# Packed loads of a, q, k on one queue, v narrowed on the chip, states in two operations: a gated-attention and MLP kernel on one core

## The chip, the cores and the metric

The kernel runs on one core of a Trainium2 chip. The metric is the device time of one execution in microseconds; a profiled execution gives in addition a trace and a span (first to last instruction). Engines are TensorE (PE), its weight load (PEld), VectorE (DVE), ScalarE (ACT), GpSimd (POOL) and SyncE (SP). The program fixes the order of each engine's instructions.

## The reference, cut to what matters

```python
# q, k, v, alpha: [4 batches, 8 heads, 768 tokens, 48] f32
for t in range(S):
    state = alpha[:, :, t, :, None] * state + einsum('bhd,bhe->bhde', k[:, :, t], v[:, :, t])
    y[:, :, t] = einsum('bhd,bhde->bhe', q[:, :, t], state)
x = y as [3072 tokens, 384]
h = x @ w_in                                   # 384 -> 2048
g = 0.5 * h * (1 + tanh(sqrt(2/pi) * (h + 0.044715 * h**3)))
return g @ w_out                               # 2048 -> 384
```

## The kernel before

The tokens are cut in six chunks of 128, the four batches in two pairs, which gives twelve "pairs" (0 to 11), in the order chunk by chunk. For each pair the kernel loads a (alpha), q, k and v. It takes ln of a, sums it along the tokens with a matmul (`cum`), forms `b = exp(cum)` and its inverse, scales q and k with them (`qp`, `kp`) and transposes both. Then come the attention inside the chunk (`at`, masked to `atm`), y (`yps`), k-times-v for the carried state (`kv`), and the two layers of the MLP (`hT`, then `acc`).

Python code at build time lists tasks with assumed durations in ns (the table `W`), simulates the engines, and emits the instructions in the resulting order. So a duration in `W` costs nothing on the chip, but it decides the order. Parts that the change touches:

```python
W = dict(..., st=1400, st0=700, ..., strip=2120, cast=1500, ...)
LOADS = ('gatea0', 'v0', 'gatek0', 'in 0', 'pk1', 'in 1', 'in 2', 'v1', ...)   # POOL's loads, in order
RINGS = (('a', 0, 0, 'SP'), ('a', 0, 2, 'ACT'), ..., ('q', 1, 3, 'SP'))        # 20 pieces, on SP and ACT
BUFS = dict(..., ot=6, bend=8, a=4, q=4, k=4, v=6)
...
def load(self, n, c, i, lo=0, hi=2):            # v: f32 in memory, bf16 on chip, so a casting DMA
    ...
    u[n] = self.tile(n, [C, 2, H, D], BF16 if n == "v" else F32)
    (nc.sync if e == "SP" else nc.gpsimd).dma_start(...)
...
def carry(self, u, i, c, b):                    # state = (kv + old) * b at the chunk's end
    for o in range(2):                          # the two diagonal blocks of a head pair, 64 lanes each
        ps, fs = slice(64 * o, 64 * o + 64), slice(D * o, D * o + D)
        acc = kv[ps, :, fs]
        if c > 0:
            s = ...
            nc.vector.tensor_tensor(s[ps], acc, old[ps, :, fs], op=ALU.add)
            acc = s[ps]
        nc.vector.tensor_tensor(new[ps, :, fs], acc, u["bend"][ps, i, :, None].to_broadcast(...), op=ALU.mult)
```

A buffer is reused in turn: with `a=4` the a of pair 4 can be issued only when pair 0 is done with its a. `gatea0` is a tiny POOL copy that waits until a of pair 0 has landed and so holds back the loads behind it.

## Time and profile before

| | before |
|---|---|
| time, median of 3 runs | 185.55 us (184.06 to 185.78) |
| span of the profiled run | 183.2 us |
| v, k of pair 1, loads of later pairs, weights | POOL, 0.6 to 1.3 us of issuing each |
| loads of pairs 0 and 1 (a, q; k of pair 0) | SP and ACT, in pieces |

```profile
33.10 2.76 PE L516 MATMUL acc<-w_out,gT 128*128 128x384 bf16 x16
...
54.55 0.34 PE L441 MATMUL kv<-v,kp 128*128 128x96 bf16 x4
```

Apart from 0.4 us for gT, PE's waits lie in the first 24 us. No wait for `v` appears in that view.

### The profile page before, as it was taken

To read this page: it belongs to the slowest core of one execution; us is meant where nothing else is said; L and a number is where in the kernel's file an instruction comes from. 1 tells how busy PE (TensorE), PEld (TensorE's weight loads), DVE (VectorE), ACT (ScalarE), POOL (GpSimd) and SP (SyncE) were. 2 spreads that over 40 slices of the span, in tenths; PEclk is the share of its full clock that TensorE was granted. 3 is DMA by queue.
4 is the path that set the end of the run, shared out by engine and by line. 5 is a ranking of instruction groups with operands and counts; after the bars stand their busy time and mean duration, and the time that the engine had idled before them with its cause. 6 is when DMAs were issued, how large, how long until landed. Compare 5 with 4: busy or idle time off the path is not lost.

```text
span 183.2 us, 4630 instructions
## 1 busy us (share of the span) xinstructions
PE 175.7 (96%) x1861; PEld 129.3 (71%) x1861; DVE 104.2 (57%) x232; ACT 135.6 (74%) x310; POOL 60.9 (33%) x68
## 2 busy tenths in 40 slices
PE   7887999999999999999999999999999999999993
PEld 2465869666686787687688769678677677686873
DVE  7775954065969896597499798298644715000000
ACT  3666969873888789859799768899789884491941
POOL 2595837975545755564750200000000000000000
PEclk9999999999999999999999999999999999999999
DMA  5999999999999999999999955753271290311102
GB/s 155 187 242 211 187 231 214 204 202 174 195 281 183 169 229 197 181 225 205 180 213 235 179 171 100 104 115 67 52 170 46 43 202 4 88 43 47 43 0 86
DMA packets 51206, 27.76 MB, mean 151 GB/s; under 512 B 38833, under 2 KB 48241, under 8 KB 51185
## 3 DMA queue, kind: packets, MB, share of 16 engines
q0 software_dynamic: 32096, 17.70, 69.0%
q1 hardware_dynamic: 18512, 9.38, 21.5%
q10 hardware_dynamic: 576, 0.39, 0.7%
q8 instruction: 14, 0.23, 0.6%
q14 instruction: 8, 0.06, 0.1%
HBM read 25.17 MB, written 4.72 MB: 163 GB/s over the span
## 4 chain that ended last, share of the span: by engine, by line
PE 85%; DMA 6%; ACT 3%; DVE 2%; SPq 1%; ACTq 1%; issue 0%
PE acc L516 34%; PE hT L497 31%; PE at L424 4%; PE qkT_ps L364 4%; PE yps L473 3%; DMA a<-in_alpha_dram 2%; PE yps L470 2%; DMA q<-in_q_dram 2%; PE cum L320 2%; PE kv L441 2%; DMA qkT<-kp 2%; PE xT_ps L487 1%; DVE atm L431 1%; ACT L503 1%; PE cum L322 1%; SPq L247 1%
## 5 line engine op out<-in xcount | busy, mean ns | idle before, releaser
L497 PE MATMUL hT<-xT,w_in 128*128 128x256 bf16 x576 | 70.1, 273 | 0.4 <-ACT gT L503 0.4
L503 ACT ACTIVATE gT<-hT 128x256 bf16<-128x256 f32 x192 | 63.4, 387 | 8.6 <-PE hT L497 8.3
L516 PE MATMUL acc<-w_out,gT 128*128 128x384 bf16 (+1 forms) x400 | 68.8, 319 | 0.0
L497 PEld LDWEIGHTS <-w_in 128*128 128x128 bf16 x576 | 54.0, 98 | 8.0 <-issue 0.6
L516 PEld LDWEIGHTS <-gT 128*128 128x128 bf16 x400 | 36.8, 98 | 19.6
L431 DVE TENSOR_TENSOR atm<-at,ut 128x512 bf16<-128x512 f32 x48 | 30.9, 685 | 15.0 <-PE at L424 14.5
L354 DVE TENSOR_TENSOR qp<-q,b 128x768 bf16<-128x768 f32 (+1 forms) x15 | 11.7, 794 | 18.7 <-ACT b L343 15.8
L528 ACT COPY ot<-acc 128x384 f32<-128x384 f32 (+1 forms) x18 | 8.3, 462 | 13.9 <-PE acc L516 12.6
L235 POOL DMA_DIRECT2D v<-in_v_dram x13 | 14.6, 1123 | 9.6 <-PE hT L497 2.9
L235 POOL DMA_DIRECT2D k<-in_k_dram x11 | 12.2, 1112 | 11.0 <-DVE kp L354 5.2
L343 ACT ACTIVATE b<-cum 128x768 bf16<-128x768 f32 (+1 forms) x15 | 10.2, 684 | 6.7 <-PE cum L322 3.1
L235 POOL DMA_DIRECT2D q<-in_q_dram x11 | 12.3, 1114 | 7.0 <-DMA k<-in_k_dram 1.8
L235 POOL DMA_DIRECT2D a<-in_alpha_dram x11 | 12.3, 1114 | 5.9 <-ACT gT L503 2.2
L213 ACT ACT_TABLE_LOAD x9 | 11.5, 1283 | 2.8 <-issue 2.6
L480 ACT CAST x<-yps 128x384 bf16<-128x384 f32 x16 | 7.7, 481 | 7.8 <-PE yps L473 7.6
L458 DVE TENSOR_TENSOR st<-stmp,bend 64x192 bf16<-64x192 f32 x32 | 11.3, 353 | 1.5
L354 DVE TENSOR_TENSOR kp<-k,binv 128x768 bf16<-128x768 f32 (+1 forms) x15 | 11.8, 792 | 0.2
L456 DVE TENSOR_TENSOR stmp<-kv,st 64x192 f32<-64x192 f32 x32 | 11.3, 352 | 1.0 <-PE kv L441 0.7
L503 ACT ACT_TABLE_LOAD x9 | 11.5, 1283 | 0.2
L222 PE MATMUL idle<-zero 128*128 128x512 bf16 x27 | 9.5, 462 | 1.2 <-DVE blk L778 1.2
L382 DVE COPY qkT<-qkT_ps 128x1024 bf16<-128x1024 bf16 (+1 forms) x13 | 8.7, 688 | 3.0 <-PE qkT_ps L364 2.9
L343 ACT ACTIVATE binv<-cum 128x768 bf16<-128x768 f32 (+1 forms) x15 | 10.1, 683 | 0.0
(62 smaller groups left out, 159.4 us busy)
## 6 DMA issues: line engine op xcount, KB each, us to landing
out_dram<-ot SPq DMA_DIRECT2D x23, 192.0 KB, 2.3
a<-in_alpha_dram POOLq DMA_DIRECT2D x9, 384.0 KB, 13.1
q<-in_q_dram POOLq DMA_DIRECT2D x9, 384.0 KB, 13.2
k<-in_k_dram POOLq DMA_DIRECT2D x9, 384.0 KB, 13.3
v<-in_v_dram POOLq DMA_DIRECT2D x11, 192.0 KB, 13.3
w_in<-in_moe_w_in_dram POOLq DMA_DIRECT2D x4, 384.0 KB, 7.7
w_out<-in_moe_w_out_dram POOLq DMA_DIRECT2D x4, 384.0 KB, 9.8
a<-in_alpha_dram SPq DMA_DIRECT2D x6, 96.0 KB, 3.4
```

The lines of the kernel that those rows point to most:

```text
L213: nc.scalar.add_instruction(mybir.InstLoadActFuncSet(name=nc.get_next_instruction_name(), act_func_set_id=i, engine=mybir.EngineType.Activ ...
L222: self.nc.tensor.matmul(ps, self.zero[:, 0:self.C], self.zero, start=True, stop=True)
L235: (nc.sync if e == "SP" else nc.gpsimd).dma_start(u[n][:, lo:hi].rearrange("t b h d -> t (b h) d"), src)
L343: self.nc.scalar.activation(u[n].rearrange("t i h d -> t i (h d)")[:, lo:hi], cum, AF.Exp, scale=1.0 if n == "b" else -1.0)
L354: self.nc.vector.tensor_tensor(out, rows, b, op=ALU.mult)
L382: self.copy(e)(t, ps)
L431: self.nc.vector.tensor_tensor(u["atm", i][:, o], u["at", i][o], self.ut[:, None, :].to_broadcast([self.C, self.H // 2, self.C]), op=ALU.mult)
L456: nc.vector.tensor_tensor(s[ps], acc, old[ps, :, fs], op=ALU.add)
L458: nc.vector.tensor_tensor(new[ps, :, fs], acc, u["bend"][ps, i, :, None].to_broadcast([64, H // 2, D]), op=ALU.mult)
L497: self.nc.tensor.matmul(h, self.w_in[:, j, nt * self.C:(nt + 1) * self.C], self.xT[c][:, j, lo:hi].rearrange("p g t -> p (g t)"), start=j ...
L503: return lambda e: self.nc.scalar.activation(self.gT[c % self.NG][:, nt, lo * self.C:hi * self.C], f.pop(("h", c, lo, nt)), AF.Gelu_apprx_ ...
L516: self.nc.tensor.matmul(f["acc", c, b][:, lo:hi], self.gT[c % self.NG][:, nt, b * self.C:(b + 1) * self.C], self.w_out[:, nt, lo:hi], star ...
```

## The change

The intent is a shorter head. Of the first two pairs, a, q and k come in one transfer each on SP's queue, four tokens a row, instead of pieces. A casting load has to leave from GpSimd (point 1 of the prediction's section on the Trainium skill), so v of pair 0, now on SP, comes as f32; v of pairs 0 to 3 is f32 and a copy on chip (`vb`) narrows it to bf16: for pairs 0 and 1 on DVE, for pairs 2 and 3 on POOL. The state takes two operations over all 128 lanes instead of four over 64; a small operation (`ends`) multiplies the decay with a mask of zeros and ones, so that the unwanted blocks vanish. The scheduler's durations are adapted (`st`, `strip`, `cast` and others).

```diff
-    ... st=1400, st0=700, ...      strip=2120, cast=1500, ...
+    ... st=1090, st0=545, end=110, ... strip=1850, cast=3000, ... ring=1150, vb2_pool=950, ...
-    LOADS = ('gatea0', 'v0', 'gatek0', 'in 0', 'pk1', 'in 1', 'in 2', 'v1', 'in 3', ...)
+    LOADS = ('gatev0', 'in 0', 'v1', 'in 1', 'in 2', 'in 3', 'out 0', '2a', 'out 1', '2b', ...)
-    RINGS = (('a', 0, 0, 'SP'), ('a', 0, 2, 'ACT'), ... 20 pieces)
+    RINGS = (('a', 0), ('q', 0), ('k', 0), ('a', 1), ('v', 0), ('q', 1), ('k', 1))
+    NARROW = (0, 1, 2, 3)
-    BUFS = dict(... ot=6, bend=8, a=4, q=4, k=4, v=6)
+    BUFS = dict(... ot=5, bend=3, ends=8, a=4, q=4, k=4, v=2, vb=6)
...
+    def narrow(self, u, lo, hi):
+            (self.nc.gpsimd.tensor_copy if e == "POOL" else self.nc.vector.tensor_copy)(u["vb"]..., u["v"]...)
...
-            for o in range(2):
-                ... add and multiply on 64 lanes
+                nc.vector.tensor_tensor(s, acc, old, op=ALU.add)
+            nc.vector.tensor_tensor(new..., acc..., ends, op=ALU.mult)
...
+                    narrow[lo:hi] = [s.add("vb", {"DVE": W[f"vb{n}"]} if early else {"POOL": W[f"vb{n}_pool"]},
+                                           P + 9 if early else -1, self.narrow(u, lo, hi), [loads["v", m, lo]])] * n
```

Also changed: the setup of the small masks takes three operations instead of a dozen, the memsets of the states fall away, and `cum` of pair 0 takes a buffer apart from pair 1's.

## The prediction

> **What bounds the kernel now.** The page comes first: PE (TensorE) is busy for 96% of the 183.2 us span. The busy time of each engine in stretches then splits PE's time; its columns are the stretch, its length, and busy us (instructions) of PE, weight load, DVE, ACT and POOL, then granted clock, DMA share and GB/s.
>
> ```profile
> PE 175.7 (96%) x1861; PEld 129.3 (71%) x1861; DVE 104.2 (57%) x232; ACT 135.6 (74%) x310; POOL 60.9 (33%) x68
> ```
>
> ```profile
> 0.00:17.20 17.20, 13.47 (x128) 7.66 (x129) 11.96 (x50) 9.07 (x23) 9.94 (x21) 1.00 1.04 199
> 17.20:28.70 11.50, 11.24 (x142) 8.83 (x139) 8.10 (x18) 9.25 (x24) 7.59 (x10) 1.00 1.46 205
> 28.70:175.00 146.30, 145.76 (x1550) 108.78 (x1549) 84.17 (x165) 115.64 (x261) 43.39 (x39) 1.00 0.91 148
> ```
>
> The same view for the fill matmuls (tile "idle") gives 7.96, 1.19 and 0.38 us. So real PE work is 5.5 of the first 17.2 us, 10.05 of the next 11.5, and nearly all of the 146 us after. An improvement can come only from the first 28.7 us. A loss can come from anything that makes PE, which runs its instructions in order, wait later.
>
> The chain that ended last, in order of time, says what the head waits for (start, us, what):
>
> ```profile
> 1.68 3.91 DMA q<-in_q_dram
> 5.60 0.31 SPq L247
> ...
> 6.94 4.41 DMA a<-in_alpha_dram
> 11.45 0.53 ACT la L301
> ...
> 15.38 1.02 DVE qp L354 x2
> 16.41 0.28 DVE xT L491
> ```
>
> The SP queue issues a of pair 1 only when q of pair 0 has landed; a of pair 1 arrives at 11.35. The program order agrees: from the ninth hardware transfer on, each waits for the eighth before it. By issue plus time to landing, the last piece of q of pair 1 comes at 15.2. DVE is in order, so its scaling at 15.38 holds the two xT copies behind it, and layer 1 begins at 17.21.
>
> The POOL queue decides my number. Its timeline from 38 us (start, us, instruction, idle before):
>
> ```profile
> 40.52 1.16 POOL L235 DMA_DIRECT2D v<-in_v_dram  x1 [1.19 <-issue]
> 42.55 1.15 POOL L235 DMA_DIRECT2D a<-in_alpha_dram  x1 [0.87 <-issue]
> 44.71 1.15 POOL L235 DMA_DIRECT2D q<-in_q_dram  x1 [1.00 <-DVE atm L431]
> 46.13 1.15 POOL L235 DMA_DIRECT2D k<-in_k_dram  x1 [0.28 <-issue]
> 48.26 1.15 POOL L235 DMA_DIRECT2D v<-in_v_dram  x1 [0.98 <-issue]
> ...
> 61.66 1.15 POOL L235 DMA_DIRECT2D a<-in_alpha_dram  x1 [1.02 <-DMA k<-in_k_dram]
> 63.15 1.15 POOL L235 DMA_DIRECT2D v<-in_v_dram  x1 [0.34 <-PE acc L516]
> ```
>
> POOL issues one strip per 2.1 us, not per 1.15 us. Landings (issue plus time to landing of each single transfer) are: a of pair 3 40.2, q 42.2, k 44.4, v 45.8, then a of pair 4 48.0, up to v of pair 5 at 62.9. Each issue above follows by 0.3 us the landing of the transfer seven places before it: v of pair 4 at 40.52 after 40.2, a of pair 5 at 42.55 after 42.2, v of pair 8 at 63.15 after 62.9. POOL is held at the pace of the data. Today this is free, since only loads for later pairs stand in that queue.
>
> **What the Trainium skill says.** (1) "DMA: Bandwidth & Descriptors", section SWDGE vs HWDGE vs iDMA: a transfer that casts must be issued from GpSimd. The trace agrees, with every v on POOL at 192 KB against 384 KB of the others; so v on SP must stay f32, hence the copies. (2) "VectorE: DVE Perf Modes", section The TRN2 errata: an f32 tensor_tensor of N elements a lane takes (N+151)/0.96 ns. That is 357 for 192 and 557 for 384; the trace has 353 (st, 64x192) and 552 (kp, 128x384). (3) "GPSIMD Engine Reference", section 3.1: 1.8 cycles an element at 1.2 GHz as a best loop. I take from it an estimate of 0.58 us for a copy of 128x384 and 1.15 for 128x768; no such copy is in this trace. (4) "TensorE: Matmul & The Clock Gate", Part 1: after an idle window of about 3.4 us PE runs at half clock for about as long. The first nine fills agree (4.02 us, 0.45 each, against 0.22 modelled later); no later stall here is long enough to show it again.
>
> **The change part by part.**
>
> *Head.* Eight a/q pieces, four k and eight more of pair 1 on SP, ACT and POOL become seven transfers on SP with no slot wait (seven are under eight). Issues took 0.31 to 0.46 us, so all are out by about 3.9 us. The stretch from 2 to 3 us moved 284 GB/s, so 393 KB take 1.4 us: a of pair 0 at about 3.9, q 5.3, k 6.6, a of pair 1 8.0. For v, with 192-byte rows, I take 2.0 us (about 200 GB/s, the rate of such rows on POOL): 10.1. Then q at 11.5 and k at 12.9. q thus comes 3.7 us earlier than now. But DVE takes in v of pair 0 (two copies, 0.6) ahead of four masks (0.65 each, until about 13.6), then qp, xT, two kp, xT (0.55+0.35+1.05+0.35): layer 1 starts near 16.0, 1.1 us earlier.
>
> *States.* 72 operations of 0.353 us (25.4) become 36 of 0.557 plus ten ends of about 0.11 (21.2): 4.2 us off DVE, which is 57% busy and does not bound. PE idles only 0.54 us between 28.7 and 175 us, so this is worth at most a few tenths.
>
> *Narrowing.* For pairs 0 and 1 it is on DVE, 4 x 0.3. For pairs 2 and 3 the scheduler gave it to POOL, and the built program shows where:
>
> ```
> POOL: a3 q3 k3 v3 a4 q4 [narrow 2, first half] k4 v4 a5 q5 k5 [narrow 2, second half]
>       v5 a6 q6 k6 v6 v7 a7 v8 [narrow 3] ...
> PE:   y of pair 2, both halves, and kv of pair 3 wait for POOL
> ```
>
> Digits are pairs. The copy for pair 3 stands behind 19 loads, which POOL issues at the pace of landings. When does it run?
>
> - The first weight transfer is gated on v of pair 0 (10.1), so issued at 10.3 against 8.19 now, but with less beside it: landing about 15.0 (now 15.5). From there one queue. Landings now give 1.9 us a weight part, and 3.3 and 3.5 us for the two halves of pair 2; v in f32 adds 0.5 to each. Up to a of pair 3: seven weight parts 13.2, v of pair 1 1.9, pair 2 7.8, a of pair 3 2.1, or 25.0, so 40.0 (now 40.2).
> - v of pair 3 as f32 costs 0.6 more than as bf16. From a of pair 3 to v of pair 5 it was 22.7, so 23.3 now: 63.3. v of pair 8 is issued 0.3 later, and 1.15 + 1.15 us on the copy is done: **65.9**.
> - PE reaches kv of pair 3 at 54.55 now. In the new order six layer-1 matmuls (0.66 us) move behind it, and the head gives 1.1: 52.8 without stalls.
> - The second half of pair 2 waits as well: its copy stands behind k of pair 5, issued when v of pair 3 landed (46.2+0.3+1.15, plus the copy, 48.3). y needs it at 45.69 now, 44.6 then: 3.7 us of stall, so kv of pair 3 is reached at 56.5 and waits 9.4 more.
>
> The end moves by 65.95 - 54.55 + 0.66 = 12.1 us, since PE has no slack afterwards to win it back. A stall of 9 us ought to cost about 1.5 us of half clock besides. The gains at the head vanish: kv of pair 3 is tied to POOL, not to PE.
>
> **Rivals.** *A: the intended gain.* If the POOL copies come in time, only the head counts: -1.1 us, about 184.4. For it: the scheduler placed the copies so that they are in time by its own costs. Against it: those costs let POOL issue every 1.1 us, while the trace shows 2.1. *B: a milder POOL stall.* If transfers run faster with all hardware loads gone early (say 1.85 instead of 2.06 us a strip), the copy is done near 63 and the end moves by about 9 us. The strips after 38 us already run without competing loads, which speaks against much of this. *C: v of pair 0 late on the hardware queue.* It holds DVE and the gate of all weights; a microsecond late there delays layer 1 and, through the weights, the whole POOL queue by as much. That adds to my case. *D: DVE blocked by v of pair 1* (a copy waiting until about 17 us): at most 1 us, swallowed by the later wait.
>
> **How the numbers follow.** The span becomes 183.2 + 12.1 + 1.5 = 196.8; the timed median stands 2.35 above the span now, giving 199. I lean a little towards B and say 197.5. The low end, 190, is strips of 1.6 us from 39 us on (copy done at 59.8, end 5.9 later), no clock loss, and a time only 0.9 above the span, as in the fastest run; the high end, 203, is C on top. Rival A keeps 9 in 100, split between a small and a large gain.
>
> **What would show it.** Right: two POOL copies late, the one of 128x768 near 65 us; PE waiting on POOL for some 4 us before y of pair 2 (about 44 to 48) and 9 us before kv of pair 3 (about 57 to 66); a lower PE clock just after; a of pair 1 landed by about 8, layer 1 started near 16; state operations near 0.55 us. Wrong: that copy done before 55 us, no PE wait on POOL, and PE idle after 28 us still around half a microsecond; or strips landing clearly faster than one per 2 us.

## More of the kernel before

The prediction shows the busy line, three stretches, the chain of waits and POOL's timeline. What is to be added here is the view of waits for PE alone (engine, tile, source line, who it waited for, then us in total, times, and the longest), and two places of PE's timeline (start, us, instruction): the first layer-2 matmul, and `kv` of pair 3, which the prediction turns on.

```profile
...
PE qkT_ps L364 <- DVE xT L491: 1.0, 1, 1.0
...
PE hT L497 <- ACT gT L503: 0.4, 1, 0.4
```

## The result, and the profile after

The changed kernel took **196.69 us** median (195.45 to 196.9, four runs), the kernel before 185.43 us in the same measurement (184.06 to 185.78). The ratio is 1.0622 (95% interval 1.057 to 1.0674). Ratios here are the mean time of one kernel's fast runs over that of the other's of the same rounds, so not quite the ratio of the medians. The result is correct. The profiled span went from 183.2 to 195.1 us.

First the page of the changed kernel, its busy line and two of its rows of 40 slices (4.9 us each, tenths).

```profile
PE 177.3 (91%) x1856; PEld 130.4 (67%) x1856; DVE 99.3 (51%) x196; ACT 134.2 (69%) x307; POOL 59.0 (30%) x65
...
PE   7896999993961999999999999998999999999993
...
PEclk9999999999996699999999999999999999999999
```

PE is less busy (91% instead of 96%), and both rows say where: slices 10, 12 and 13, between 44 and 63 us, and a low clock in slices 13 and 14, 58 to 68 us. The same stretches as in the prediction, of the changed kernel:

```profile
0.00:17.20 17.20, 15.05 (x148) 9.21 (x149) 11.08 (x38) 11.17 (x26) 7.96 (x17) 1.00 0.85 213
17.20:28.70 11.50, 9.55 (x124) 7.69 (x122) 7.90 (x17) 8.65 (x24) 6.58 (x9) 1.00 1.18 208
28.70:175.00 146.30, 135.94 (x1454) 100.67 (x1453) 80.31 (x142) 105.72 (x234) 44.50 (x41) 0.98 0.78 148
```

PE's idle time in the long stretch went from 0.54 to 10.36 us. In the head PE got more real work done before 17.2 us (15.05 minus 7.55 us of fill matmuls, so 7.5 us against 5.5) but idled 1.95 us just after it. Now who kept PE waiting (waits of PE, changed kernel):

```profile
PE kv L442 <- POOL vb L345: 5.8, 1, 5.8
PE yps L482 <- POOL vb L345: 3.4, 1, 3.4
PE at L425 <- DVE qkT L383: 1.8, 1, 1.8
...
PE hT L506 <- ACT gT L512: 1.2, 3, 0.6
```

Two single waits on the narrowing copies make 9.2 us in all. The timelines put them in their places; PE's first (start, us, instruction, idle before it), then POOL's.

```profile
32.34 2.76 PE L525 MATMUL acc<-w_out,gT 128*128 128x384 bf16 x16
...
48.47 0.36 PE L482 MATMUL yps<-vb,atm 128*128 128x48 bf16 x8 [3.37 <-POOL vb L345]
...
62.54 0.48 PE L442 MATMUL kv<-vb,kp 128*128 128x96 bf16 x4 [5.80 <-POOL vb L345]
...
66.37 1.18 PE L525 MATMUL acc<-w_out,gT 128*128 128x384 bf16 x4
```

```profile
47.90 0.52 POOL L345 CAST vb<-v 128x384 bf16<-128x384 f32 x1
...
60.52 1.14 POOL L243 DMA_DIRECT2D vb<-in_v_dram  x1 [0.40 <-issue]
61.65 0.83 POOL L345 CAST vb<-v 128x768 bf16<-128x768 f32 x1
```

Both copies run the moment the load ahead of them in POOL's queue is issued. The view names no releaser for POOL's gap before the load of 60.52 ("issue"), but that load follows by 0.3 us a landing, that of v of pair 5 at 60.21, as in the prediction's reading of the trace before. The v that the copy of 61.65 reads had landed at 46.45; the copy waited for its turn only. Last, stretches of 2 us after the long stall (columns as above, granted clock third from the end):

```profile
58.00:60.00 2.00, 0.00 (x0) 0.00 (x0) 0.07 (x1) 0.00 (x0) 1.07 (x2) 1.00 1.37 242
60.00:62.00 2.00, 0.00 (x0) 0.00 (x0) 0.00 (x0) 0.00 (x0) 1.60 (x3) 0.58 1.06 216
62.00:64.00 2.00, 1.46 (x13) 1.21 (x13) 0.91 (x2) 0.31 (x1) 1.58 (x2) 0.50 1.68 175
64.00:66.00 2.00, 2.00 (x13) 1.22 (x13) 0.20 (x1) 0.91 (x4) 1.15 (x1) 0.50 2.40 156
```

While PE stood still its clock fell to 0.50, and it worked at that speed until some 66 us (0.72 in the next 2 us, then 1.00).

**Where the 11.9 us of span come from.** The first layer-2 matmul (`acc`) starts at 32.34 us, 0.76 earlier than before (33.10). From there to the end it takes 162.76 us instead of 150.1: 12.66 more. The two waits give 3.37 + 5.80 = 9.17; the low clock about 2.1 (by a comparison under `warm` below, from single profiles); PE's waits on ACT for gT grew from 0.4 to 1.2, so 0.8. That makes 12.1; some 0.6 us is not itemised. `early` below, with the same order of PE and neither wait, needs 151.4 us for this stretch: 11.4 less than the changed kernel and 1.3 more than the kernel before. So the two waits and the low clock (11.3) cover what the copies' place costs, and the 0.8 and the 0.6 belong to what `early` keeps, which is PE's new order, or to the difference of single executions.

### The profile page after: what moved, and what is told of

Read it like the earlier page. It is cut to its first block, busy times and chain, and to the rows that moved or that the text cites. A ratio compares the mean times of both kernels' runs of the same rounds, so it can differ in the third digit from the quotient of the medians.

```text
span 195.1 us, 4539 instructions
## 1 busy us (share of the span) xinstructions
PE 177.3 (91%) x1856; PEld 130.4 (67%) x1856; DVE 99.3 (51%) x196; ACT 134.2 (69%) x307; POOL 59.0 (30%) x65
## 4 chain that ended last, share of the span: by engine, by line
PE 64%; DMA 13%; POOL 10%; issue 5%; ACT 2%; DVE 2%; SPq 1%; POOLq 0%; DVEq 0%
PE acc L525 27%; PE hT L506 25%; DMA w_out<-in_moe_w_out_dram 6%; DMA w_in<-in_moe_w_in_dram 4%; DMA v<-in_v_dram 3%; PE at L425 3%; PE yps L482 2%; POOL k L243 2%; PE qkT_ps L365 2%; POOL vb L243 2%; PE yps L479 2%; POOL a L243 2%; POOL q L243 2%; PE cum L314 1%; SPq L240 1%
## 5 line engine op out<-in xcount | busy, mean ns | idle before, releaser
L512 ACT ACTIVATE gT<-hT 128x256 bf16<-128x256 f32 x192 | 62.9, 388 | 17.3 <-PE hT L506 16.8
L506 PE MATMUL hT<-xT,w_in 128*128 128x256 bf16 x576 | 71.7, 276 | 1.3 <-ACT gT L512 1.2
L506 PEld LDWEIGHTS <-w_in 128*128 128x128 bf16 x576 | 54.7, 99 | 9.7 <-issue 1.7
L525 PEld LDWEIGHTS <-gT 128*128 128x128 bf16 x400 | 36.8, 98 | 19.7 <-issue 0.5
L537 ACT COPY ot<-acc 128x384 f32<-128x384 f32 (+1 forms) x16 | 7.4, 460 | 20.0 <-PE acc L525 19.1
L243 POOL DMA_DIRECT2D a<-in_alpha_dram x11 | 12.2, 1107 | 22.9 <-ACT la L297 19.7
L355 DVE TENSOR_TENSOR qp<-q,b 128x768 bf16<-128x768 f32 (+1 forms) x15 | 11.8, 792 | 13.9 <-ACT b L337 13.8
L215 ACT ACT_TABLE_LOAD x9 | 11.5, 1283 | 0.9 <-PEq L818 0.7
L482 PE MATMUL yps<-vb,atm 128*128 128x48 bf16 x192 | 8.8, 183 | 3.4 <-POOL vb L345 3.4
L512 ACT ACT_TABLE_LOAD x9 | 11.5, 1283 | 0.2
L425 PE MATMUL at<-qkT 64*128 64x128 bf16 x192 | 9.9, 222 | 1.8 <-DVE qkT L383 1.8
L464 DVE TENSOR_TENSOR stmp<-kv,st 128x384 f32<-128x384 f32 x16 | 8.8, 550 | 5.4 <-PE kv L442 5.4
L489 DVE CAST x<-yps 128x384 bf16<-128x384 f32 x11 | 6.1, 555 | 9.7 <-PE yps L482 9.7
L425 PEld LDWEIGHTS <-qkT 64*128 64x128 bf16 x192 | 5.6, 95 | 7.3 <-issue 7.2
L442 PE MATMUL kv<-vb,kp 128*128 128x96 bf16 x64 | 4.7, 215 | 5.8 <-POOL vb L345 5.8
## 6 DMA issues: line engine op xcount, KB each, us to landing
vb<-in_v_dram POOLq DMA_DIRECT2D x8, 192.0 KB, 11.5
```

The lines of the kernel that those rows point to most:

```text
L215: nc.scalar.add_instruction(mybir.InstLoadActFuncSet(name=nc.get_next_instruction_name(), act_func_set_id=i, engine=mybir.EngineType.Activ ...
L243: dma(u[t][:, lo:hi].rearrange("t b h d -> t (b h) d"), src.rearrange("b h s d -> s (b h) d")[c * C:(c + 1) * C])
L355: self.nc.vector.tensor_tensor(out, rows, b, op=ALU.mult)
L425: nc.tensor.matmul(at[o][:, p, :], t[sl, 1, p, :], t[sl, 0, p, :], start=True, stop=True)
L464: nc.vector.tensor_tensor(s, acc, old, op=ALU.add)
L482: nc.tensor.matmul(y[:, h, :], u["atm", i][:, h % 2, h // 2, :], u["vb"][:, i, h, :], start=c == 0, stop=True, skip_group_check=True)
```

## The experiments

Theory: the place of the POOL copies in POOL's queue costs the time. Rivals: the narrowing itself is too much work wherever it runs; or the loads at the head cost it; or the states do.

**`early`: the same copies, further forward in POOL's order.** Nothing else moves; PE and DVE keep their order.

```diff
         order = self.s.order()
+        first, second, third = [t for t in order if t.kind == "vb" and t.engine == "POOL"]
+        order.remove(third);  order.insert(order.index(second), third)
+        order.remove(second); order.insert(order.index(first) + 1, second)
```

> The changed kernel with the three copies on POOL kept, but moved forward in POOL's own order: the second half of pair 2 right behind its first half, the copy of pair 3 ahead of v of pair 5 instead of behind v of pair 8. PE's and DVE's orders are the same. Theory (the copies' place in a queue that goes at the pace of landings): the copy of pair 3 is done near 49 us, PE waits on POOL for nothing, span about 182.3, time about 0.5% under the kernel before (0.995). Rival 1 (the copies on POOL are slow or fight DVE for SBUF): waits remain, above 190. Rival 2 (f32 v overloads the transfers): the stall remains in another place, above 188. Rival 3 (states or loads did it): no change, 196.

Measured: 185.84 us, ratio 1.0042 (0.9989 to 1.0096), span 183.8. POOL's timeline shows the three copies in two entries:

```profile
38.31 0.97 POOL L345 CAST vb<-v 128x384 bf16<-128x384 f32 x2
...
47.35 1.38 POOL L345 CAST vb<-v 128x768 bf16<-128x768 f32 x1
```

No wait of PE on POOL is left. The work is the same, on the same engine; only its turn changed, and the whole loss of the change is gone. The gain at the head that I expected on top (0.995) is missing; the last four runs come back to it.

**`vb8`: the dose.** Two more buffers for `vb` (and fewer for two others, to make room) let the scheduler put two more loads of v ahead of the last copy.

```diff
-    x=3, ot=5, ... v=2, vb=6
+    x=2, ot=4, ... v=2, vb=8
```

> The changed kernel with two more bf16 buffers for v (vb 8, paid with ot 4 and x 2). PE's and DVE's orders are the same; the scheduler puts two more loads of v ahead of the copy of pair 3 in POOL's order. Theory: two more landings at about 1.8 us each, so the copy is done near 66 us instead of 62.5 and the end moves by about 3.5 us: ratio 1.08, time about 200. Rival (a buffer was missing): more buffers help, under 196.

Measured: 200.8 us, ratio 1.0844 (1.0775 to 1.0913), span 198.7. In the timelines of PE and POOL:

```profile
66.19 0.48 PE L442 MATMUL kv<-vb,kp 128*128 128x96 bf16 x4 [7.60 <-POOL vb L345]
```

```profile
65.31 0.83 POOL L345 CAST vb<-v 128x768 bf16<-128x768 f32 x1
```

Two more loads in front put the copy 3.66 us later (65.31 against 61.65), and the span grew by 3.6. PE's wait before y of pair 2 was 3.59 us here, and the clock was 0.50 already after it (48 to 52 us); the wait before `kv` of pair 3 swallows that. From this `kv` to the end the two profiles agree: 132.5 us here, 132.6 in the changed kernel. More buffers made the kernel slower, since they allowed more loads to stand ahead of a copy that PE needs.

**`n012` and `n01`: no narrowing for pair 3, then none for pairs 2 and 3.** The v that isn't narrowed comes with a casting load, as before.

```diff
-    NARROW = (0, 1, 2, 3)
+    NARROW = (0, 1, 2)        # n012
+    NARROW = (0, 1)           # n01
```

> The changed kernel with v of pair 3 cast by its transfer again (no copy for it); pairs 0 to 2 still narrowed on chip. PE's order is the same. Theory: the first wait of PE (3.4 us before y of pair 2) stays, the second one (5.8) and the low clock after it (about 2 to 3 us) go: span about 186.0, ratio about 1.015. Rival 2 (f32 v overloads the transfers): most of the loss stays.

Measured: 188.62 us, ratio 1.0187 (1.0139 to 1.0235; at a threshold of 2% this counts as unclear), span 187.4. One wait of PE on POOL remains:

```profile
48.71 0.36 PE L482 MATMUL yps<-vb,atm 128*128 128x48 bf16 x8 [2.67 <-POOL vb L345]
```

> The changed kernel with v of pairs 2 and 3 cast by their transfers again; everything else kept, pairs 0 and 1 narrowed on DVE. Theory: no POOL wait; what is left is the gain of the head and the states, about 0.9 us measured at 28 us: span about 182.3, ratio 0.995. Rival 3 (states or coalesced loads cost time): ratio above 1.02.

Measured: 185.64 us, ratio 1.0042 (0.9975 to 1.011), span 184.4; no wait on POOL. So pair 3 costs about 8 us of time and pair 2 about 3, which is the split of the two waits plus the clock. But the gain at the head that I expected here did not come: the first layer-1 matmul started at 17.46 us in this profile (15.79 in the changed kernel's), with k of pair 0 landing at 8.6 us (7.5 there) and a wait of PE of 0.5 us for a weight. A first miss; the head is taken up again below.

**`warm`: is the low clock a cost of its own?** 24 fill matmuls before `kv` of pair 3 keep PE busy while it waits.

```diff
         def emit(e):
+            if (u["m"], i) == (3, 0):
+                self.fill(24)(e)
             kv = u["kv", i] = self.tile("yk", [C, H // 2, 2 * D], F32, "kv")
```

> The changed kernel with 24 fill matmuls in PE's order right before kv of pair 3, so about 5.2 us of work on zeros into the 5.8 us for which PE waits there; they write a scratch bank that nobody reads. The copy of pair 3 is still done at 62.5. Theory (part of the loss is a lower clock after a long idle stretch): granted clock back to 1.0 after the wait, the 3.8 us that kv to the second at took become about 2.0, the end about 2.2 us earlier: about 194.3, ratio 1.049. Rival (the slow matmuls after the wait have another cause, such as waiting for ACT): no change, 1.062.

Measured: 195.83 us, ratio 1.0597 (1.0538 to 1.0656); span 194.9. The expected gain in time is not there. The profile tells more:

```profile
57.55 5.35 PE L224 MATMUL idle<-zero 128*128 128x512 bf16 x24
...
64.46 0.33 PE L444 MATMUL kv<-vb,kp 128*128 128x96 bf16 x4 [1.56 <-POOL vb L345]
```

The granted clock stays at 1.00. The next `acc` starts at 66.53: from `kv` to it 2.07 us pass instead of 3.83 (62.54 to 66.37), and from `kv` to the end 194.9 - 64.46 = 130.44 instead of 195.1 - 62.54 = 132.56: 2.1 us less. But in this execution the copy came at 63.58, 1.9 us later than in the changed kernel's profile, and that took the gain back. The profiled execution took 197.81 us, the slowest of its four; the other three took 195.32 to 196.16, against 196.56 to 196.9 for three of the changed kernel's four (the fourth took 195.45) in an earlier measurement. The mean granted clock of the four executions was 0.989 to 1.000, against 0.965 to 0.982. So the mechanism shows in the clock and in the profile; its worth in time, 1 to 2 us, is not resolved by these runs.

**`dve_all`: all narrowing on DVE.** A test of the rival that the work, not its place, is at fault.

```diff
-    {"DVE": W[f"vb{n}"]} if early else {"POOL": W[f"vb{n}_pool"]}
+    {"DVE": W[f"vb{n}"]} if early else {"DVE": W[f"vb{n}"]}
```

> The changed kernel with the copies of pairs 2 and 3 given to DVE too, none on POOL. Theory: no PE wait on a copy, because DVE's queue goes at the pace of PE's work and not of transfers; some 1.4 us more DVE work, which is 51% busy: within 1% of the kernel before, like the kernel with these copies left out (1.004). Rival (any copy that stands in line for a late strip stalls PE, whichever engine): DVE waits for v of pair 3 (landed 46.4) and the ratio is above 1.015.

Measured: 194.77 us, ratio 1.052 (1.0454 to 1.0586), span 193.1. The theory's number failed and the rival's held, though not its mechanism: v of pair 3 had landed at 46.35 us, and no wait of PE on a copy appears. The scheduler made another program of it. Its DVE timeline has the copy of pair 3 late, near the end of a long row of other work:

```profile
68.62 0.55 DVE L345 CAST vb<-v 128x768 bf16<-128x768 f32 x1
```

DVE ran without a pause from 62.9 to 69.7 us. PE took pair 4's `kv` at 63.98, before pair 3's at 71.94 (before: 54.55), and idled 3.4 us in small pieces between 60 and 75 us. Its clock was 0.81 there, and also 0.85 from 17.2 to 28.7 us. So the time went in small waits and at a low clock in another order of PE. Whether the late copy is what causes this is not shown, and the run does not tell what a well placed copy on DVE would cost.

**`coal`: the loads at the head alone, without v on SP.** No narrowing at all; a, q, k of pairs 0 and 1 in one transfer each, v from POOL as before. The states stay in two operations, with the new durations.

```diff
-    LOADS = ('gatev0', 'in 0', 'v1', ...)
+    LOADS = ('gatea0', 'v0', 'gatek0', 'in 0', 'in 1', 'in 2', 'v1', ...)
-    RINGS = (('a', 0), ('q', 0), ('k', 0), ('a', 1), ('v', 0), ('q', 1), ('k', 1))
-    NARROW = (0, 1, 2, 3)
+    RINGS = (('a', 0), ('q', 0), ('k', 0), ('a', 1), ('q', 1), ('k', 1))
+    NARROW = ()
```

> The changed kernel without any narrowing: v always cast by its transfer from POOL, in the old order of the POOL queue behind gates on a and k of pair 0; a, q, k of the first two pairs stay single transfers on SP and the states stay in two operations. Theory: v on SP (2048 short rows) is what held the sixth issue on SP for 4 to 5 us and k, a and v late in the head; without it q of pair 1 is issued by 5 us and lands near 11, first layer-1 matmul near 16.0, ratio 0.990 to 0.998. Rival (single transfers gain nothing): 1.00 or above.

Measured: 186.53 us, ratio 1.0097 (1.005 to 1.0144), span 186.9: a miss. PE's timeline:

```profile
10.74 0.40 PE L365 MATMUL qkT_ps<-ident,kp 128*128 128x128 bf16 x4 [2.83 <-DVE kp L355]
```

q of pair 0 had landed at 5.9 us, but k of pair 0 only at 10.0, though it was issued at 2.20. By 5.4 us SP had issued a, q and k of pair 1 as well, and POOL v of pair 0 at 5.02, so five transfers were under way together; which of them held k back is not separated. (The kernel before also issued v at 5.06, and had k of pair 0, in pieces, in time for its first scaling at 7.88 us.) After the wait of 2.83 us PE ran at 0.50 of its clock from 12 to 14 us, and layer 1 began at 19.74 (17.21 before). This execution took 188.68 us, the slowest of the six; the other five took 186.39 to 187.07 at a mean clock of 1.00, so the low clock is not part of the median. One transfer each is not by itself quicker to the first use.

**`states_old`: the states alone.** The kernel before with two operations for the state and `ends`, nothing else; the scheduler keeps its old durations (`st=1400, st0=700`), so that the order hardly moves.

> The kernel before with the two-operation states alone, and the scheduler's costs left as they were, so that PE's order stays nearly the same. Theory: DVE busy falls by about 4 us (104.2 to 100), PE idle after 28 us stays around half a microsecond, and the time moves by less than 0.3%: ratio 0.998 to 1.001. Rival (states on the path): ratio below 0.99.

Measured: 183.8 us (183.44 to 185.26), ratio 0.9937 (0.9895 to 0.9978), span 182.3. More than expected, and the best kernel. DVE's busy time falls from 104.2 to 96.8 us, of which the states' memsets in the setup are 1.7. The first `acc` starts at 32.58 us instead of 33.10, and from there to the end it takes 149.72 instead of 150.1.

**Four more runs: where does the head's gain go?** Three theories were put to the test: that DVE's copy of v of pair 1, which waits for its load and holds the copy of the transposed q and k behind it, costs the head a microsecond; that the *new durations* in `W` gave a worse order; and both.

```diff
# early_fix: early, and on DVE the two copies of v of pair 1 behind the next copy out of PSUM
+        for t in [t for t in order if t.kind == "vb" and t.engine == "DVE"][2:]:
+            to = next(x for x in order[order.index(t):] if x.kind == "ev" and x.engine == "DVE")
+            order.remove(t); order.insert(order.index(to) + 1, t)
# early_old: early with the old durations   # early_fix_old: both edits
-    st=1090, st0=545, end=110
+    st=1400, st0=700, end=10
# states: states_old with the new durations
-    st=1400, st0=700, end=10
+    st=1090, st0=545, end=110
```

> The run with the narrowing copies moved forward on POOL (ratio 1.0042, span 183.8) plus one more move: on DVE the two copies of v of pair 1, which waited there 1.66 us for v until 17.98 and held the copy of the transposed q and k behind them, now stand behind that copy. Theory: this wait is in the head's path (PE waited 1.4 us for that copy), so most of it comes off the end: PE's wait falls to 0.5 us or less, the block of 42 layer-1 matmuls starts about 1 us earlier, ratio 0.998 (0.995 to 1.000). Rival: PE runs into the next thing that is late, a part of w_in or the first kv of pair 1, and the wait only changes its name: ratio 1.004, the block of 42 starts as before.

Measured: 185.73 us, ratio 1.0047 (1.0008 to 1.0087), span 183.4. The rival held. PE's wait of 1.4 us for the copy of q and k is gone, but the next operation waits in its place:

```profile
19.20 0.34 PE L442 MATMUL kv<-vb,kn 128*128 128x96 bf16 x4 [0.81 <-DVE kn L398]
```

The first `acc` came at 31.56 us instead of 32.40, and half of that was lost again by the end.

> The run with the narrowing copies moved forward on POOL, with the scheduler's durations of the state operations put back to those of the kernel before (two long operations, no cost of the ends); operations and data are the same, PE's order differs in 1159 lines of the listing. Theory: the new durations gave a worse order; PE's two waits for ACT of 0.18 and 0.61 us at 110 and 124 us, which the kernel before and the run with the old durations do not have, are gone, ratio 0.999 (0.996 to 1.001). Rival: order is not what holds it, and the ratio stays at 1.004.

Measured: 185.0 us, ratio 1.0004 (0.9965 to 1.0044), span 184.3 with a clock of 0.85 from 17.2 to 28.7 us in that profile. PE's waits for gT at 110 and 124 us are gone, as the theory said.

> Both of the other edits together: copies forward on POOL, v of pair 1 behind the copy of the transposed q and k on DVE, old durations for the scheduler. If both theories hold, this is the head's gain of the change without its stall: ratio 0.993 (0.990 to 0.997), about as good as the two-operation states alone (0.9937). If both fail: 1.004.

Measured: 184.88 us, ratio 0.9976 (0.9935 to 1.0016), span 182.4; one of the six runs, 187.25 us, lies over 1.5% above the fastest and is left out of the ratio. A miss: 0.990 to 0.997 was expected. PE's head now waited for a weight instead: layer 1 began at 16.98 after 0.90 us on `w_in`.

> The kernel before with the states in two operations, and the scheduler told the new durations (the run with old durations gave 0.9937, span 182.3); the PE listing differs in 97 lines from that run. Theory: the gain of that run comes from 4 us less on DVE ahead of layer 1 and in the head, whatever the order: ratio 0.994 again. Rival: it comes from a luckier order or a luckier landing: with the new durations the waits for ACT of some 0.8 us appear and the ratio is 0.998 to 1.000.

Measured: 184.93 us, ratio 0.9997 (0.9962 to 1.0031), span 183.4. The rival held: the operations are those of `states_old`, the gain is not there. PE's timeline has two waits that `states_old` lacks, 0.18 us at 109.64 and this one:

```profile
123.79 2.45 PE L506 MATMUL hT<-xT,w_in 128*128 128x256 bf16 x21 [0.62 <-ACT gT L512]
```

What follows from the four is best read from one table, the time from the first `acc` to the end of the span, in us:

| kernel | old durations | new durations | ratios (old, new) |
|---|---|---|---|
| before plus two-operation states | 149.7 | 151.0 | 0.9937, 0.9997 |
| copies early | 150.6 | 151.4 | 1.0004, 1.0042 |
| copies early, v of pair 1 moved | 150.0 | 151.8 | 0.9976, 1.0047 |
| before | 150.1 | | |

In all three rows the order that comes of the new durations is 0.8 to 1.8 us longer. `n01` and `coal`, also with new durations, took 151.2 and 151.4. Each single pair of ratios has overlapping intervals, and the first two pairs were not measured together; the same sign three times, with the same two waits in the profiles, makes it likely, not certain. The new durations are nearer to what the trace shows (two operations of 0.55 us), and still give the worse order.

## Why the prediction was right

**The step that carried it held.** The place of the two POOL copies behind loads that POOL issues at the pace of landings was read from the built order and the trace before, and the changed kernel does what was said: each issue comes about 0.3 us after a landing of the transfer seven places before (v of pair 8 issued at 60.52, v of pair 5 landed at 60.21). `early` shows by an intervention that the place is the cause, `vb8` shows the dose.

**The sizes compensated, and that was luck.** The time was 196.69 against a predicted 197.5, but the terms were off in both directions. With the copy done at 62.5, the prediction's own sum gives 62.5 - 54.55 + 0.66 = 8.6 us instead of 12.1.

| term | predicted | measured |
|---|---|---|
| from a of pair 3 to v of pair 5, landings | 23.3 us | 19.7 (40.5 to 60.2) |
| copy 128x768 on POOL | 1.15 | 0.83 |
| that copy done | 65.9 | 62.5 |
| PE's wait before y of pair 2 | 3.7 | 3.37 |
| PE's wait before `kv` of pair 3 | 9.4 | 5.80 |
| low clock after it | 1.5 | about 2.1 |
| more waits for ACT in the new order | not foreseen | 0.8 |
| timed median over the span | 2.35 | 1.6 |

The mis-sized term is the first: the strips landed one per 1.79 us, not per 2.06. Strips "clearly faster than one per 2 us" stood in the prediction among the signs of being wrong, and that sign came true. Rival B had named the size (1.85, copy done near 63). I had spoken against it since "the strips after 38 us already run without competing loads", which did not settle the size. In the profile the DMAs moved 236 GB/s from 28.7 to 45 us, against 201 before. But `states_old` and `states`, whose loads are those of the kernel before in the same order, moved 225 and 224 there, and from a of pair 3 to v of pair 5 they took 21.6 and 19.7 us, against 22.7 in the kernel before. So the same loads run at the changed kernel's pace in one execution and slower in another: the faster strips need no cause in the change, rival B's reason for them is not shown, and what I took for a constant was read from one trace. The low end of my range (strips of 1.6 us) was not far away. What I had not foreseen filled the gap: the clock was worth more, and PE waited more for ACT, probably through the order that the new durations gave.

**The head.** First layer 1 at 15.79 us (predicted 16.0), a of pair 1 at 8.8 in that profile (8.0 predicted), so the gain was real. "All are out by about 3.9 us" was wrong. SP's timeline has 0.61 to 0.74 us per issue, and the sixth (q of pair 1, behind v with its many short rows) held SP from 4.21 to 8.71 us:

```profile
3.55 0.62 SPq L243 DMA_DIRECT2D v<-in_v_dram  x1
4.21 4.50 SPq L240 DMA_DIRECT2D q<-in_q_dram  x1
```

The landings of q and k of pair 1 were still close, 11.8 and 12.8 (11.5 and 12.9 predicted); with that step wrong, this too is luck. Rival D came true, with a wait of 1.8 us where I had allowed 1, and the later stall swallowed it. But when the stall is taken away the head's gain does not reappear in the time: `n01` and `early` are at 1.0042, and with both orders mended 0.9976, whose interval holds 1. Rival A was therefore too hopeful on its own terms, too: "only the head counts: -1.1 us" was not found in any run with the new loads.

**The states.** I gave 21.2 us of DVE time for the new operations; the trace has 21.5 (16 of 0.558, 16 of 0.550, 4 of 0.550 and ten ends of 0.167). "At most a few tenths" was an underestimate by the ratio of `states_old`, and right by that of `states`; if the reading of the table above holds, the difference is order.

**What stays open**: why the pace of the same loads differs between executions; the worth of the clock in time, since `warm` did not resolve it; whether a copy on DVE in the right place would be free; and what held k of pair 0 in `coal`.

## What to carry to other kernels

Before an operation is put on an engine that also issues loads, read from the trace at which pace that engine gets through its queue: here GpSimd advanced by one load per landing, and two copies of 0.5 and 0.8 us, the longer one behind 19 loads, cost some 11 us of the kernel's time (196.69 against 185.84), and nothing that was measured a few places earlier. More buffers can make that worse, since they let more loads stand in front. When a kernel's order comes from a scheduler with assumed durations, run a change once with the durations left alone: what is gained by the operations and what is lost by the order are then two numbers.

## What the Trainium skill lacked or had wrong

- "DMA: Bandwidth & Descriptors", section Queues, rings and completion order, does not say how many transfers issued by GpSimd may be under way before the next issue is held; other pages speak of a buffer of descriptors that can be full, without a number of transfers. Once the queue was held (from 40.5 us), nearly every issue of a strip came about 0.3 us after the landing of the one seven places before, in the kernels before and after (40.52 after 40.2; 60.52 after 60.21). What holds it is not shown.
- The same page, section Anatomy of one DMA, calls descriptor generation "small, variable", for GpSimd; the issue of a strip took 0.9 to 1.2 us here. For SP no page gives a cost. SP's issues took 0.61 to 0.74 us each, the one behind v of pair 0 (192-byte rows) 4.50 us, and 1.20 us in the run without v on that queue. That the short rows are the cause is my reading; no run separates them from v itself.
- "GPSIMD Engine Reference", section 3.1: its best loop gave my estimates of 0.58 and 1.15 us for a narrowing copy. Measured were 0.52 (128x384) and 0.83 (128x768) in the changed kernel, though 1.38 for the latter in `early`. The section also states a faster rate, for the shortest loop bodies, and does not say which a copy is; so my choice of the rate was off, not the page.
- "TensorE: Matmul & The Clock Gate", Part 1, has the clock fall after an idle window of about 3.4 us that runs freely. Here 5.80 us idle brought it to 0.50, and 3.37 us did not, but 3.59 us did in `vb8` and 2.83 us in `coal`. `early` and `early_old` had nearly the same idle time from 18 to 20 us (PE busy 0.58 and 0.54 of 2 us) and only the second fell to 0.50. That it varies from run to run agrees with the page; an idle time under 3.4 us is not a safe one.
